# Softmax of a band attention before an MoE feed-forward: the guard becomes a second summed column, both query tiles are scaled by one reciprocal in one step, and the sink weights are copied out

## The chip, the cores and the metric

One core of one Trainium2 chip runs the whole kernel as a single launch. The metric is device time in microseconds of that core. The kernel before took 796.38, 807.41 and 798.26 us in three runs, median 798.26 us. The profiled execution took 798.38 us. Differences under about 2% (16 us) count as no change here.

## The reference, cut to what matters

```python
scores = scale * np.matmul(q, k.transpose(0, 1, 3, 2))        # 4 batches, 8 heads, 768 x 768, head size 64
keep = is_sink | in_window                                     # first 4 keys, or the last 128 keys
scores = np.where(keep, scores, -1000000000.0)
scores = scores - np.max(scores, axis=-1, keepdims=True)
a = np.exp(scores)
a = a / (np.sum(a, axis=-1, keepdims=True) + 1e-09)
attn = np.matmul(a, v)
x = attn.transpose(0, 2, 1, 3).reshape(3072, 512)
gate = 1.0 / (1.0 + np.exp(-(x @ w_gate)))                     # w_gate, w_val: 512 x 1536
out = (gate * (x @ w_val)) @ w_out                             # w_out: 1536 x 512
```

The inputs are float64 for the weights and float32 for q, k and v, and the result is float32. The kernel reads the float64 weights as pairs of 32-bit words and decodes them on the chip.

## The kernel before, in words

**Attention.** A unit is one batch, one head and T = 2 tiles of 128 query rows. There are 96 units, in the order batch, group of two tiles, head. For a query tile, a 128-wide band and 4 sink columns are kept, so a row of weights has KW = 132 columns. For each of the two tiles TensorE makes the scores (tile `a`), VectorE merges the two diagonal halves, adds the mask, scales and takes the row's extreme (`top`, line 743; it writes `P` and `negm_all`), and ScalarE takes the exponential of `P` in place with the row sums accumulated into `rs` (`exp`, line 751). Then for both tiles together the guard 1e-9 is added to `rs` (line 764, GpSimd or VectorE), VectorE takes the reciprocal (line 771), each tile's 128 band columns are multiplied by it (lines 773 to 789, GpSimd, ScalarE or VectorE), and the 4 sink columns of both tiles are multiplied into `psk`, which collects them over the 8 heads (line 792, VectorE or GpSimd). TensorE transposes the band part of `P` (`turn`, line 810), ScalarE copies it to `wt`, GpSimd splits it at the diagonal with two selects (`split`, line 816), and TensorE multiplies by `v` (`pv`, line 872). After the eighth head `join` (line 928) adds the sink part from `psk` and writes the split activations `XH` and `XL`, of which a ring of 6 tiles is kept. The first 16 units are "plain": they use unsplit float32 operands.

**Weights.** 36 `decode` steps (line 995) each load 512 KB of float64 words into `wst`, turn them into `w` by one ScalarE step, one conversion of `wst` on ScalarE, VectorE or GpSimd (line 1019) and two VectorE steps, and split `w` into a high part (`wgh`, `wvh`, `woh`) and a low one (`wgl`, `wvl`, `wlo`). The low part of the output weights goes to DRAM (`wol_d`) and is loaded again for each use (`wol`).

**Feed-forward.** `feed` (line 1061) takes chunks of 2 or 3 tiles of tokens. For each of the 12 slices of 128 hidden columns TensorE makes 12 matmuls for the gate and 12 for the value (into `m`), ScalarE takes the tanh (`th`), VectorE multiplies, `gh` and `gl` split the product, and 3 matmuls a tile accumulate into `o`.

**What sets the order.** Each step is put on a list with `plan.op` (line 264): a priority, the engines that may do it with a time in ns for each, and the tiles that it reads and writes. `Plan.run` (line 288) goes through a clock of its own, gives each free engine the first waiting step that it may do, and multiplies the times on VectorE, ScalarE and GpSimd by 1.2 before 200 us (line 393). The instructions are then emitted in that order, and each engine's order is kept. A step's time in the table so sets where it and all later ones stand, and on which engine. Where TensorE would stay too idle before 130 us, the plan puts a filler matmul (`m<-ident`, `warm`, line 649) into its queue. `P` and `rs` have two buffers, `a` has three.

Of the kernel before, what the change touches and what calls it, by code (L numbers as in the profile page):

```python
# [9 lines left out]
F32 = mybir.dt.float32  # L10
# [5 lines left out]
ALU = mybir.AluOpType  # L16
AX = mybir.AxisListType
# [3 lines left out]
NS = 4  # L21
# [50 lines left out]
BUFS = {}  # L72
# [361 lines left out]
def kernel(  # L434
# [13 lines left out]
    nc = tc.nc  # L448
# [11 lines left out]
    KW = 128 + NS  # L460
# [17 lines left out]
    plan = Plan()  # L478
# [72 lines left out]
    def tile(shape, dtype, tag, bufs, pool=None):  # L551
        return Tile(pool or p1, shape, dtype, tag, bufs)
# [89 lines left out]
    plan.op(-1, [("G", 250, places)], w=[mk])  # L642


    MS = [ps.tile([128, 512], F32, name=f"m{i}") for i in range(BUFS["m"])]
    assert max(map(max, MT)) * 128 + 128 <= 512
    PE.matmul(MS[0][:, 384:512], lhsT=ident, rhs=ident, start=True, stop=True)
# [44 lines left out]
    def attend(u, b, h, t0, T, XR, XS, PSK):  # L692
# [32 lines left out]
            PSK[0] = tile([128, T, H, NS], F32, "psk", BUFS["psk"])  # L725
        psk = PSK[0]
        P = tile([128, T, KW], F32, "P", BUFS["P"])
        rs = tile([128, 4], F32, "rs", BUFS["P"])
        for t in range(T):
            sc = tile([128, 512], F32, "a", BUFS["a"], ps)  # L730
            first = t0 + t == 0
            n = KW if first else KW + 128

            def qk(t=t, sc=sc, n=n):
                s0 = max(t + prev - 1, 0) * KW
                K = D if plain else 128
                for i, (qq, kk) in enumerate(pairs):
                    PE.matmul(
                        sc()[:, 0:n], lhsT=qq()[0:K, t * 128 : t * 128 + 128],
                        rhs=kk()[0:K, s0 : s0 + n], start=i == 0, stop=i == len(pairs) - 1,  # L740
                    )

            def top(t=t, sc=sc, first=first):
                if not first:
                    V.copy_predicated(out=sc()[:, 0:128], mask=tri, data=sc()[:, KW : KW + 128])
                V.tensor_tensor_reduce(
                    out=P()[:, t], in0=sc()[:, 0:KW], in1=am[min(t0 + t, 2)], op0=ALU.add,
                    op1=ALU.min, scale=-SCALE, scalar=3.0e38, accum_out=negm_all[:, u, t : t + 1],
                )

            def exp(t=t):
                A.activation(
                    out=P()[:, t], in_=P()[:, t], func=AF.Exp, bias=negm_all[:, u, t : t + 1],
                    scale=-1.0, accum_out=rs()[:, t : t + 1],
                )

            plan.op(u, [("PE", 90 + 1.667 * n if plain else 10 + 2 * mac(n), qk)], qk_reads, [sc, (P, t)], busy=0.5 if plain else 0.9)
            plan.op(
                u, [("V", 290 if first else 600, top)],
                [sc, (MASKS, 3), (MASKS, min(t0 + t, 2))], [sc, (P, t)],  # L760
            )
            plan.op(u, [("A", 460, exp)], [], [(P, t), (rs, t)])

        def guard(E):
            return lambda: E.tensor_scalar(
                out=rs()[:, 0:T], in0=rs()[:, 0:T], scalar1=1.0e-9, scalar2=None, op0=ALU.add
            )

        plan.op(u, [("G", 400, guard(G)), ("V", 250, guard(V))], [], [rs])
        plan.op(  # L770
            u, [("V", 120, lambda: V.reciprocal(out=rs()[:, 0:T], in_=rs()[:, 0:T]))], [], [rs]
        )
        for t in range(T):
            plan.op(
                u, [
                    ("V", 390, lambda t=t: V.tensor_scalar(
                        out=P()[:, t, 0:128], in0=P()[:, t, 0:128], scalar1=rs()[:, t : t + 1],
                        scalar2=None, op0=ALU.mult,
                    )),
                    ("A", 320, lambda t=t: A.mul(  # L780
                        out=P()[:, t, 0:128], in_=P()[:, t, 0:128], mul=rs()[:, t : t + 1]
                    )),
                    ("G", 450, lambda t=t: G.tensor_scalar(
                        out=P()[:, t, 0:128], in0=P()[:, t, 0:128], scalar1=rs()[:, t : t + 1],
                        scalar2=None, op0=ALU.mult,
                    )),
                ][::-1],
                [rs], [(P, t)],
            )


        def sink_weights(E):
            return lambda: E.tensor_tensor(
                out=psk()[:, 0:T, h], in0=P()[:, 0:T, 128:KW],
                in1=rs()[:, 0:T].unsqueeze(2).to_broadcast([128, T, NS]), op=ALU.mult,
            )

        plan.op(
            u, [("V", 110, sink_weights(V)), ("G", 400, sink_weights(G))], [rs, (P, T)], [(psk, h)]
        )  # L800


# [192 lines left out]
    def decode(prio, src, hi, lo):  # L995

        n, m = src.shape[1], src.shape[2]
        st = tile([128, n, m, 2], I32, "wst", BUFS["wst"], p2)
        a = tile([128, n, m], F32, "w2", BUFS["w2"])
        ai = lambda: a().bitcast(I32)
        hw = lambda: st()[:, :, :, 1]
        plan.op(prio, [("Q", 460, lambda: Q.dma_start(out=st(), in_=src))], [], [st], dma=1456.0)
        by = lambda i: st().rearrange("p n m w -> p (n m w)").bitcast(U8).rearrange(
            "p (x b) -> p x b", b=8
        )[:, :, i]
        plan.op(  # L1010
            prio, [("A", act(512), lambda: A.mul(out=a(), in_=hw().bitcast(F32), mul=2.0**-112))],
            [(st, 0)], [a],
        )

        lw = lambda: st()[:, :, :, 0]
        three = dict(scale=1.0 / 32, bias=-31.0 / 64)
        two = dict(scalar1=1.0 / 32, scalar2=-31.0 / 64, op0=ALU.mult, op1=ALU.add)
        flat = lambda: st().rearrange("p n m w -> p (n m w)").rearrange("p (x w) -> p x w", w=2)[:, :, 0]
        plan.op(
            prio, [  # L1020
                ("A", act(512), lambda: A.activation(out=flat(), in_=by(3), func=AF.Copy, **three)),
                ("V", 700.0, lambda: V.tensor_scalar(out=flat(), in0=by(3), **two)),
                ("G", 1000.0, lambda: G.tensor_scalar(out=flat(), in0=by(3), **two)),
            ],
            [], [(st, 1)],
        )
        plan.op(
            prio, [("V", vec(512), lambda: V.scalar_tensor_tensor(
                out=ai(), in0=ai(), scalar=3, in1=lw(), op0=ALU.logical_shift_left,
                op1=ALU.bitwise_or,  # L1030
            ))],
            [(st, 1)], [a],
        )
        plan.op(
            prio, [("V", vec(512), lambda: V.scalar_tensor_tensor(
                out=ai(), in0=hw(), scalar=-2147483648, in1=ai(), op0=ALU.bitwise_and,
                op1=ALU.bitwise_or,
            ))],
            [(st, 0)], [a],
        )  # L1040
        copy(prio, 512, hi, a, [a], [hi])
        rest(prio, 512, lo, a, hi, [a, hi], [lo])
# [210 lines left out]
```

## Time and profile before

| | |
|---|---|
| median of three runs | 798.26 us |
| profiled execution | 798.38 us, its span 796.7 us |
| TensorE matmul (PE) | busy 773.8 us, 97% of the span |
| VectorE (DVE) | 513.4 us, 64% |
| GpSimd (POOL) | 437.5 us, 55% |
| ScalarE (ACT) | 403.2 us, 51% |
| mean granted clock of TensorE | 0.992 of 2.4 GHz |

A share of the span is a mean over stages. The span begins 1.4 us before the first matmul and ends with the last store. The profile's time of a matmul runs from its start to its modelled end, and neighbours overlap, so a busy share of 1.0 says that TensorE had no gap, not how fast it streams. A filler counts as busy.

### The profile page before, as it was taken

To read this page: it belongs to the slowest core of one execution; us is meant where nothing else is said; L and a number is where in the kernel's file an instruction comes from. 1 tells how busy PE (TensorE), PEld (TensorE's weight loads), DVE (VectorE), ACT (ScalarE), POOL (GpSimd) and SP (SyncE) were. 2 spreads that over 40 slices of the span, in tenths; PEclk is the share of its full clock that TensorE was granted. 3 is DMA by queue.
4 is the path that set the end of the run, shared out by engine and by line. 5 is a ranking of instruction groups with operands and counts; after the bars stand their busy time and mean duration, and the time that the engine had idled before them with its cause. 6 is when DMAs were issued, how large, how long until landed. Compare 5 with 4: busy or idle time off the path is not lost. (4 is left out here: it accounts for less than half of the span.)

```text
span 796.7 us, 14763 instructions
## 1 busy us (share of the span) xinstructions
PE 773.8 (97%) x4540; PEld 702.8 (88%) x4540; DVE 513.4 (64%) x1550; ACT 403.2 (51%) x1190; POOL 437.5 (55%) x602
## 2 busy tenths in 40 slices
PE   7999999999999999999999999999999999999996
PEld 5677798878999999998999999999999999999995
DVE  5787798998799988899871388885861331111110
ACT  4786777766767767676640256664740210011001
POOL 3676798887667778668761267673751221111211
PEclk8999999999999999999999999999999999999999
DMA  5667777763645544444441235343311121113111
GB/s 162 198 190 207 191 213 253 231 201 115 192 126 151 149 107 122 119 116 112 142 113 40 57 104 133 104 129 111 92 45 42 41 79 40 40 40 92 39 42 57
DMA packets 98421, 94.33 MB, mean 118 GB/s; under 512 B 43168, under 2 KB 77984, under 8 KB 98336
## 3 DMA queue, kind: packets, MB, share of 16 engines
q1 hardware_dynamic: 98336, 93.32, 41.1%
q8 instruction: 38, 0.62, 0.3%
q14 instruction: 47, 0.39, 0.1%
HBM read 83.85 MB, written 9.44 MB: 117 GB/s over the span
## 5 line engine op out<-in xcount | busy, mean ns | idle before, releaser
L488 DVE SCALAR_TENSOR_TENSOR th<-th,m 128x384 f32<-128x384 f32 (+1 forms) x108 | 54.6, 505 | 184.3 <-PE m L488 182.9
L488 POOL TENSOR_TENSOR gl<-th,gh 128x384 fp32r<-128x384 f32 (+1 forms) x65 | 65.5, 1008 | 195.4 <-DVE gh L488 183.0
L488 ACT ACTIVATE th<-m 128x384 f32<-128x384 f32 (+1 forms) x108 | 49.1, 454 | 209.4 <-PE m L488 207.5
L488 POOL TENSOR_SCALAR_AFFINE_SELECT wt<-wt 128x512 fp32r<-128x512 f32 (+3 forms) x192 | 121.5, 633 | 42.6 <-DVE wt L488 24.2
L488 PE MATMUL m<-XH,wvh 128*128 128x384 f32 (+1 forms) x432 | 140.1, 324 | 0.4 <-ACT th L488 0.4
L488 PE MATMUL m<-XH,wgh 128*128 128x384 f32 (+1 forms) x432 | 140.3, 325 | 0.0
L488 PE MATMUL m<-XH,wvl 128*128 128x384 f32 (+1 forms) x432 | 137.7, 319 | 0.0
L488 PE MATMUL m<-XL,wvh 128*128 128x384 f32 (+1 forms) x432 | 137.6, 319 | 0.0
L488 PE MATMUL m<-XH,wgl 128*128 128x384 f32 (+1 forms) x432 | 137.5, 318 | 0.0
L488 PE MATMUL m<-XL,wgh 128*128 128x384 f32 (+1 forms) x432 | 137.3, 318 | 0.0
L488 PE MATMUL o<-woh,gh 128*128 128x512 f32 x276 | 113.0, 409 | 1.0 <-DVE total L1201 1.0
L488 PE MATMUL o<-woh,gl 128*128 128x512 f32 x276 | 109.5, 397 | 2.2 <-DVE gl L488 1.6
L488 PE MATMUL o<-wol,gh 128*128 128x512 f32 x276 | 108.8, 394 | 2.5 <-DMA wol<-wol_d 2.5
L488 ACT ACTIVATE P<-P,negm_all 128x132 f32<-128x132 f32 x192 | 77.2, 402 | 30.5 <-DVE negm_all L488 27.0
L488 PEld LDWEIGHTS m<-XH,wvh 128*128 128x128 f32 x432 | 81.7, 189 | 3.3 <-ACT th L488 0.6
L488 PEld LDWEIGHTS m<-XH,wgh 128*128 128x128 f32 x432 | 81.4, 189 | 2.1 <-issue 0.2
L488 PEld LDWEIGHTS m<-XL,wvh 128*128 128x128 f32 x432 | 81.8, 189 | 1.5
L488 PEld LDWEIGHTS m<-XL,wgh 128*128 128x128 f32 x432 | 81.5, 189 | 1.6
L488 PEld LDWEIGHTS m<-XH,wvl 128*128 128x128 f32 x432 | 81.7, 189 | 0.0
L488 PEld LDWEIGHTS m<-XH,wgl 128*128 128x128 f32 x432 | 81.3, 188 | 0.0
L488 PEld LDWEIGHTS o<-woh,gl 128*128 128x128 f32 x276 | 52.0, 188 | 16.6 <-DVE gl L488 3.5
L488 DVE CUSTOM_DVE_ANT_0 P<-a,am 128x132 f32<-128x132 f32 x192 | 56.2, 294 | 11.9 <-PE a L488 2.9
(115 smaller groups left out, 1619.5 us busy)
## 6 DMA issues: line engine op xcount, KB each, us to landing
wol<-wol_d SPq DMA_DIRECT2D x108, 256.0 KB, 2.7
qkT<-in_k_dram SPq DMA_DIRECT2D x120, 99.0 KB, 2.6
qkT<-in_q_dram SPq DMA_DIRECT2D x176, 64.0 KB, 2.4
wst<-in_moe_w_gate_dram SPq DMA_DIRECT2D x12, 512.0 KB, 4.3
wst<-in_moe_w_val_dram SPq DMA_DIRECT2D x12, 512.0 KB, 4.3
wst<-in_moe_w_out_dram SPq DMA_DIRECT2D x12, 512.0 KB, 4.2
vraw<-in_v_dram SPq DMA_DIRECT2D x64, 96.0 KB, 2.3
out_dram<-w SPq DMA_DIRECT2D x23, 256.0 KB, 2.5
```

The source lines that it names most:

```text
L488: return lambda *a, **kw: tc.keep_in_program_order(op(*a, **kw))
```

## The change

The guard is no longer added by an instruction. Two small tiles `sums` with two columns for each query tile are filled with 1e-9 once, before the plan begins; the exponential's accumulator overwrites the first column of a tile's pair, and one VectorE reduction adds both columns into `rs`, with the reciprocal right behind it in the same step. The scaling covers all 132 columns of both tiles: one instruction on GpSimd or VectorE, or two on ScalarE. The sink weights are then copied to `psk` by GpSimd or ScalarE. One time in the decode's table changes (GpSimd's conversion of `wst`, 1000 to 560 ns).

```diff
+    SUMS = [const.tile([128, 2, 2], F32, name=f"sums{i}") for i in range(BUFS["P"])]
+    for x in SUMS:
+        nc.gpsimd.memset(x, 1.0e-9)
...
-        rs = tile([128, 4], F32, "rs", BUFS["P"])
+        sums = Tile(SUMS, None, F32, "sums", BUFS["P"])
+        rs = tile([128, T], F32, "rs", BUFS["P"])
...
-                    scale=-1.0, accum_out=rs()[:, t : t + 1],
+                    scale=-1.0, accum_out=sums()[:, t, 0:1],
...
-        plan.op(u, [("G", 400, guard(G)), ("V", 250, guard(V))], [], [rs])
-        plan.op(
-            u, [("V", 120, lambda: V.reciprocal(out=rs()[:, 0:T], in_=rs()[:, 0:T]))], [], [rs]
-        )
-        for t in range(T):
...
-                    ("V", 390, lambda t=t: V.tensor_scalar(
-                        out=P()[:, t, 0:128], in0=P()[:, t, 0:128], scalar1=rs()[:, t : t + 1],
...
-                    ("A", 320, lambda t=t: A.mul(
...
-                    ("G", 450, lambda t=t: G.tensor_scalar(
...
-        plan.op(
-            u, [("V", 110, sink_weights(V)), ("G", 400, sink_weights(G))], [rs, (P, T)], [(psk, h)]
         )
+        def guard():
+            V.tensor_reduce(out=rs(), in_=sums()[:, 0:T], axis=AX.X, op=ALU.add)
+            V.reciprocal(out=rs(), in_=rs())
+
+        plan.op(u, [("V", 320, guard)], [sums], [rs])
+        def norm(E):
+            return lambda: E.tensor_tensor(
+                out=P(), in0=P(), in1=rs().unsqueeze(2).to_broadcast([128, T, KW]), op=ALU.mult
+            )
+        def norm_each():
+            for t in range(T):
+                A.mul(out=P()[:, t], in_=P()[:, t], mul=rs()[:, t : t + 1])
+        plan.op(
+            u, [("G", 800, norm(G)), ("A", T * 350, norm_each), ("V", 380, norm(V))], [rs], [P]
+        )
+        gather = lambda: psk()[:, 0:T, h]
+        plan.op(
+            u, [
+                ("G", 230, lambda: G.tensor_copy(out=gather(), in_=P()[:, :, 128:KW])),
+                ("A", 250, lambda: A.copy(out=gather(), in_=P()[:, :, 128:KW])),
+            ],
+            [P], [(psk, h)],
+        )
...
-                ("G", 1000.0, lambda: G.tensor_scalar(out=flat(), in0=by(3), **two)),
+                ("G", 560.0, lambda: G.tensor_scalar(out=flat(), in0=by(3), **two)),
```

Counted over the whole program, the order moves these. VectorE loses 80 sink products, 43 guards and 11 scalings, and gains 96 reductions, 13 scalings of both tiles and 5 conversions of `wst`. GpSimd loses 53 guards, 45 scalings and 16 sink products, and gains 31 scalings of both tiles and 39 sink copies. ScalarE has 104 scalings instead of 136, 57 sink copies and 6 conversions of `wst` fewer. Of other steps, 12 differences `kl` and 5 `gl` go from VectorE to GpSimd. TensorE has 66 fillers instead of 69, each of them two matmul records, and its other work is the same in number.

Of the first 29 units' work, VectorE loses 23 sink products, 10 guards and 4 scalings, and gains 29 reductions, 2 scalings of both tiles and the 5 conversions. GpSimd loses 19 guards, 11 scalings and 5 sink products, and gains 9 scalings of both tiles and 12 copies. ScalarE has 36 scalings instead of 41, 17 copies, and 14 conversions instead of 20.

VectorE at the first units, before (`ISA P` is the masked extreme, `tri` the merge mask, `wst` and `w` the decode):

```order
L488 ISA P_230,negm_all<-a_220,am_86 128x132
L488 ISA negm_all 128x1
L488 TENSOR_SCALAR wst_205<-wst_205 128x512
L488 COPY_PREDICATED a_228<-tri,a_228 128x128
L488 ISA P_230,negm_all<-a_228,am_87 128x132
L488 ISA negm_all 128x1
L488 RECIPROCAL rs_218<-rs_218 128x2
L488 SCALAR_TENSOR_TENSOR w_241<-w_241,wst_205 128x512
L488 TENSOR_TENSOR psk_255<-P_215,rs_218 128x2x4
L488 SCALAR_TENSOR_TENSOR w_241<-wst_205,w_241 128x512
```

and now:

```order
L488 ISA P_233,negm_all<-a_223,am_86 128x132
L488 ISA negm_all 128x1
L488 TENSOR_SCALAR wst_209<-wst_209 128x512
L488 TENSOR_REDUCE rs_245<-sums_90 128x2
L488 RECIPROCAL rs_245<-rs_245 128x2
L488 COPY_PREDICATED a_231<-tri,a_231 128x128
L488 ISA P_233,negm_all<-a_231,am_87 128x132
L488 ISA negm_all 128x1
L488 SCALAR_TENSOR_TENSOR w_242<-w_242,wst_209 128x512
L488 SCALAR_TENSOR_TENSOR w_242<-wst_209,w_242 128x512
L488 TENSOR_REDUCE rs_272<-sums_91 128x2
```

The first unit's reciprocal stands right behind the first conversion of `wst`, where the merge and the extreme of the second unit stood ahead of it before, and no sink product follows.

GpSimd at the same place, before (`vsp` belongs to the sink values, `wt` to the transposed weights):

```order
L488 TENSOR_TENSOR vsp<-w_190,vsp 32x512
L488 TENSOR_SCALAR rs_218<-rs_218 128x2
L488 TENSOR_SCALAR wst_209<-wst_209 128x512
L488 TENSOR_SCALAR wst_213<-wst_213 128x512
L488 TENSOR_SCALAR rs_234<-rs_234 128x2
L488 AFFINE_SELECT wt_267<-wt_267 128x128
L488 AFFINE_SELECT wt_267<-wt_267 128x2x128
```

and now:

```order
L488 TENSOR_TENSOR vsp<-w_194,vsp 32x512
L488 TENSOR_TENSOR P_219<-P_219,rs_245 128x264
L488 COPY psk_257<-P_219 128x2x4
L488 TENSOR_SCALAR wst_217<-wst_217 128x512
L488 AFFINE_SELECT wt_268<-wt_268 128x128
L488 AFFINE_SELECT wt_268<-wt_268 128x2x128
```

The guards are gone, the first unit's scaling has moved here from ScalarE, and one of two conversions has gone to ScalarE.

TensorE up to the second unit's transposes, before (`m_90<-ident` is the filler, `ident,P` the transposes of a unit, `qkT` the scores):

```order
L488 MATMUL m_90<-ident 128x128 x5
L488 MATMUL a_261<-ident,P_215 128x128 x2
L488 MATMUL a_265<-qkT_193 128x132
L488 MATMUL a_271<-qkT_193 128x260
L488 MATMUL m_90<-ident 128x128 x5
```

and now:

```order
L488 MATMUL m_94<-ident 128x128 x4
L488 MATMUL a_259<-ident,P_219 128x128 x2
L488 MATMUL m_94<-ident 128x128
L488 MATMUL a_266<-qkT_197 128x132
L488 MATMUL a_270<-qkT_197 128x260
L488 MATMUL m_94<-ident 128x128 x4
```

One filler has moved behind the first unit's transposes and one has gone.

## Rows read from the trace of the kernel before

**Rows 1.** The page's head, its busy times by engine, and two rows of its 40 slices of about 20 us: TensorE's busy tenths and the granted clock in tenths.

```profile
span 796.7 us, 14763 instructions
...
PE 773.8 (97%) x4540; PEld 702.8 (88%) x4540; DVE 513.4 (64%) x1550; ACT 403.2 (51%) x1190; POOL 437.5 (55%) x602
...
PE   7999999999999999999999999999999999999996
...
PEclk8999999999999999999999999999999999999999
```

**Rows 2.** Busy time of each engine in three stretches, with the number of instructions, the granted clock, the DMA engines' share and GB/s.

```profile
0.00:60.00 60.00, 53.18 (x291) 39.67 (x292) 44.12 (x153) 39.82 (x114) 34.38 (x59) 0.94 0.62 184
60.00:200.00 140.00, 132.47 (x876) 115.56 (x875) 122.88 (x295) 100.86 (x277) 114.46 (x130) 0.99 0.67 200
200.00:790.00 590.00, 587.62 (x3376) 547.45 (x3375) 346.37 (x1105) 261.33 (x800) 288.70 (x415) 1.00 0.34 92
```

**Rows 3.** What TensorE waited for between 60 and 200 us: us in total, times, longest.

```profile
PE o L488 <- DMA wol<-wol_d: 2.5, 2, 1.3
PE o L488 <- DVE gl L488: 1.6, 3, 0.7
PE a L488 <- DVE xr L488: 0.8, 2, 0.5
PE a L488 <- DVE negm_all L488: 0.7, 2, 0.4
PE a L488 <- DVE wt L488: 0.4, 1, 0.4
```

**Rows 4.** The fillers in the groups of instructions of the whole span (count of records, busy us, mean ns, idle before), and the stretch 80 to 90 us in the columns of Rows 2.

```profile
L488 PE MATMUL m<-ident 128*128 128x128 f32 x138 | 24.8, 320 | 1.6 <-POOL ident masks.py:199 1.4
...
80.00:90.00 10.00, 8.63 (x44) 6.71 (x44) 6.68 (x20) 6.13 (x20) 6.31 (x9) 0.83 0.83 221
```

**Rows 5.** VectorE's groups of the softmax's last steps between 0 and 200 us: count, busy us, mean ns, idle of the engine just before them and what ended it.

```profile
L488 DVE TENSOR_TENSOR psk<-P,rs 128x8 f32<-128x8 f32 x23 | 12.3, 536 | 0.0
...
L488 DVE TENSOR_SCALAR rs<-rs 128x2 f32<-128x2 f32 x10 | 4.6, 461 | 2.9 <-ACT P L488 2.9
L488 DVE RECIPROCAL rs<-rs 128x2 f32<-128x2 f32 x29 | 4.5, 156 | 0.9 <-POOL rs L488 0.8
...
L488 DVE TENSOR_SCALAR P<-P,rs 128x128 f32<-128x128 f32 x4 | 2.5, 636 | 0.0
```

**Rows 6.** GpSimd's groups of the same stretch, the same columns: the steps that go, and two differences of about the new scaling's size.

```profile
L488 POOL TENSOR_TENSOR qs<-qkT,qs 64x256 fp32r<-64x256 f32 x11 | 11.1, 1005 | 2.1 <-POOL wt L488 0.9 <-POOL vhl L488 0.5
...
L488 POOL TENSOR_SCALAR P<-P,rs 128x128 f32<-128x128 f32 x11 | 9.0, 824 | 2.8 <-DVE rs L488 1.7 <-ACT wst L488 1.0
...
L488 POOL TENSOR_SCALAR rs<-rs 128x2 f32<-128x2 f32 x19 | 6.4, 335 | 7.1 <-ACT P L488 6.1
...
L488 POOL TENSOR_TENSOR kl<-qkT,kh 128x264 fp32r<-128x264 f32 x3 | 2.3, 771 | 0.2
...
L488 POOL TENSOR_TENSOR psk<-P,rs 128x8 f32<-128x8 f32 x5 | 1.6, 326 | 1.3 <-DVE rs L488 1.3
```

**Rows 7.** ScalarE's groups of the same stretch, the same columns.

```profile
L488 ACT ACTIVATE P<-P,rs 128x128 f32<-128x128 f32 x41 | 15.0, 393 | 0.7 <-DVE rs L488 0.3
L488 ACT ACTIVATE wst<-wst 128x512 int32<-128x512 uint8 x20 | 13.6, 680 | 14.1 <-DMA wst<-in_moe_w_gate_dram 8.8 <-DMA wst<-in_moe_w_out_dram 4.1 <-DMA wst<-in_moe_w_val_dram 1.0
L488 ACT ACTIVATION_READ_ACCUMULATOR P<-P,negm_all 128x1 f32 x58 | 11.0, 190 | 0.0
...
L488 ACT CAST vhl<-vraw 128x128 fp32r<-128x128 f32 x2 | 0.6, 298 | 0.9 <-PE a L488 0.9
```

**Rows 8.** The timeline at the first unit: start in us, duration, engine, operation, and in brackets the idle time before it. VectorE, then ScalarE, then TensorE.

```profile
11.13 0.43 DVE L488 TENSOR_SCALAR wst<-wst 128x512 int32<-128x512 uint8 x1 [2.94 <-DMA wst<-in_moe_w_gate_dram]
11.47 0.29 DVE L488 COPY_PREDICATED a<-tri,a 128x128 f32<-128x128 int32 x1
...
12.02 0.16 DVE L488 RECIPROCAL rs<-rs 128x2 f32<-128x2 f32 x1
...
13.11 0.68 ACT L488 ACTIVATE P<-P,rs 128x128 f32<-128x128 f32 x2
...
8.12 1.38 PE L488 MATMUL m<-ident 128*128 128x128 f32 x10
13.55 0.77 PE L488 MATMUL a<-ident,P 128*128 128x128 f32 x2 [4.05 <-ACT P L488]
```

**Rows 9.** The timeline of VectorE at three small steps that each need the one before, and of one VectorE and one GpSimd instruction that ran side by side.

```profile
4.97 0.16 DVE L488 SCALAR_TENSOR_TENSOR val<-nums 128x2 f32<-128x2 f32 x1
5.17 0.17 DVE L488 TENSOR_SCALAR val<-val 128x2 f32<-128x2 f32 x1
5.37 0.35 DVE L488 SCALAR_TENSOR_TENSOR wst<-wst,val 128x128 f32<-128x128 f32 x1
...
16.69 1.39 DVE L488 TENSOR_SCALAR P<-P,rs 128x128 f32<-128x128 f32 x1
...
16.72 1.28 POOL L488 TENSOR_TENSOR wgl<-w,wgh 128x512 fp32r<-128x512 f32 x1
```

More of the change, by code (lines that the diff above doesn't have):

```diff
@@ L761, in attend @@
             )
[L762 to L766, printed above, removed]
-            )
-        plan.op(u, [("G", 400, guard(G)), ("V", 250, guard(V))], [], [rs])
+            plan.op(u, [("A", 460, exp)], [], [(P, t), (sums, t)])
+        def guard():
+            V.tensor_reduce(out=rs(), in_=sums()[:, 0:T], axis=AX.X, op=ALU.add)
+            V.reciprocal(out=rs(), in_=rs())
@@ L772, in attend @@
         )
-        for t in range(T):
-            plan.op(
-                u, [
-                    ("V", 390, lambda t=t: V.tensor_scalar(
-                        out=P()[:, t, 0:128], in0=P()[:, t, 0:128], scalar1=rs()[:, t : t + 1],
-                        scalar2=None, op0=ALU.mult,
-                    )),
-                    ("A", 320, lambda t=t: A.mul(
-                        out=P()[:, t, 0:128], in_=P()[:, t, 0:128], mul=rs()[:, t : t + 1]
-                    )),
-                    ("G", 450, lambda t=t: G.tensor_scalar(
[L784 to L788, printed above, removed]
-            )
@@ L792, in sink_weights @@
[L792 to L796, printed above, removed]
-        plan.op(
-            u, [("V", 110, sink_weights(V)), ("G", 400, sink_weights(G))], [rs, (P, T)], [(psk, h)]
+        gather = lambda: psk()[:, 0:T, h]
+        plan.op(
+            u, [
[3 more added lines that the diff above has]
+            [P], [(psk, h)],
```

## The prediction, made before the change was run

> **What bounds the kernel now.** I read the page first: TensorE is busy for 97% of the span and no other engine reaches two thirds [rows 1]. That leaves little to win anywhere, so the question is where TensorE's gaps lie. Its row of slices shows them in the first 200 us only, so the next view is the busy time by stretch [rows 2]. From 200 to 790 us TensorE has a matmul in hand for 587.62 of 590 us: 2.4 us of gaps, while VectorE works 346 us of it. In that stretch nothing off TensorE can be worth more than 2.4 us. From 60 to 200 us TensorE is idle for 140 - 132.47 = 7.5 us, and VectorE is the fullest of the others, 122.88 of 140 us (88%). From 0 to 60 us it is idle for 6.8 us, of which 4.05 us is one wait before the first unit's transposes [rows 8]. Besides idle time there are fillers, which count as busy and do nothing: 138 records with 24.8 us [rows 4]. So the most that a better supply could give back is 7.5 + 6.8 + 24.8 = 39 us, and a good part of that is loading and decoding of weights, which the change leaves alone. Who makes TensorE wait is read from its waits between 60 and 200 us [rows 3]: VectorE for 1.6 + 0.8 + 0.7 + 0.4 = 3.5 us, the reload of `wol` for 2.5 us; GpSimd is not among them.
>
> **The change, part by part.** The first 29 units are those of the first 200 us (29 reciprocals there [rows 5]); I cost these, and the other 67 at nothing: the 2.4 us of gaps after 200 us show that feed-forward matmuls cover them. If that cover went, VectorE's 346 us in 590 would still leave it room.
>
> *VectorE.* It loses 23 sink products (12.3 us), 10 guards (4.6) and 4 scalings (2.5) [rows 5]: 19.4 us. It gains 29 reductions, which no row shows. The nearest row is the reciprocal, one input of two columns, 0.156 us; but reduction and reciprocal now stand together and the second needs the first, and two such small steps start 0.20 us apart [rows 9]. I take 0.20, so 5.8 us. The ends are 0.156 (4.5 us) and 0.461, the guard's mean here (13.4 us). It further gains 2 scalings at 0.636 (1.3 us [rows 5]) and 5 conversions of `wst` at 0.43 (2.2 us [rows 8]). Net 10.1 us less of 44.12 + 122.88 = 167.0 us, between 2.5 and 11.4 less.
>
> Why the small steps cost so much is what the choice of 0.20 hangs on. The sink product took 0.536 us for 8 columns and the guard 0.461 for 2, while the reciprocal took 0.156 [rows 5]; and a scaling on VectorE that began beside a GpSimd subtraction lasted from 16.69 to 18.08 us, that subtraction from 16.72 to 18.00 [rows 9]. These steps wait for GpSimd, and the reciprocal does not. The Trainium skill, page "SBUF — State Buffer", section "Who interferes with whom", says that VectorE instructions with two inputs in SBUF or in a two-port mode block against GpSimd's, and that a reduction never does on trn2. By that rule the reduction costs as little as the reciprocal and the sum moves by 1.3 us on VectorE, which is nothing in the time; without it, at the guard's 0.461, the relief shrinks to 2.5 us. The trace agrees for the steps that go; no row shows a reduction beside a GpSimd instruction.
>
> *A wait that moves.* GpSimd added 19 of these 29 guards and stood idle for 7.1 us ahead of them, 6.1 of it for ScalarE's exponential [rows 6]. Now every guard is VectorE's, which stops its queue (the merges and extremes of the next unit, the decode, `gl`) until the second exponential is done. If all 6.1 us arrive there, the relief is 4.0 us, otherwise up to 10.1.
>
> *GpSimd* loses 6.4 + 9.0 + 1.6 = 17.0 us and gains 9 scalings of 264 columns, at 0.771 us by the nearest difference (6.9 us; 9.0 at 1.005), and 12 copies at 0.326 (3.9 us): 6.2 us less, at least 4.1 [rows 6]. *ScalarE* loses 5 scalings (2.0 us) and 6 conversions (4.1 us); 17 copies of 8 columns lie between 0.190, its shortest step, and 0.298, a cast of 128 columns; at 0.24 they are 4.1 us [rows 7]. Net 1.9 us less, between 0.9 and 2.8. I count both at nothing: TensorE waits for GpSimd nowhere in the waits shown [rows 3], and for ScalarE only at the start [rows 8].
>
> *The start.* TensorE stands from 9.50 to 13.55 us. The first weights land at 11.13; VectorE's conversion, merge and extreme come before the reciprocal at 12.02; ScalarE scales at 13.11 [rows 8]. Now the reduction is next after the conversion, which ends at 11.56; with 0.20 + 0.16 the reciprocal is done at about 11.92, and GpSimd, which has nothing else there, scales in 0.771: 12.7, with the hand-over 12.8. **0.75 us less.** The landing at 11.13 stays ahead of it, so the two memsets at the head, which delay fillers, cost nothing. The ends are 0 (GpSimd slower) and 1.5.
>
> *Fillers.* Three fewer, 6 records of 24.8 / 138 = 0.18 us [rows 4]: **1.1 us less**, if TensorE has work in their place; 0 if it waits instead.
>
> *What TensorE waits for on VectorE.* 3.5 us between 60 and 200 us [rows 3], with VectorE relieved by 4.0 to 10.1 us of 167.0, 2 to 6%. A few per cent off an engine that is 88% busy shortens these waits without ending them: I take half, **1.75 us less**, with ends 0 and 3.5. The waits for `wol` hang on the decode and a DMA and stay. What is late next where VectorE's waits go is that reload.
>
> The sum: 0.75 + 1.1 + 1.75 = 3.6 us, from the profiled execution's 798.4 us (1.7 us more than its span) to 794.8. That execution lies 0.1 us over the median of 798.26, so **795 us** stands for both. Its own range, by the ends above, is 790 to 798.5.
>
> **The rivals.**
>
> *The supply gets well* (chance 0.12). All 7.5 us of idle time between 60 and 200 us go, the reloads with them, because VectorE runs ahead of its plan; then also the fall of the clock at 80 to 90 us, where TensorE was idle for 1.4 us and the granted clock was 0.83 of 2.4 GHz (part of the stretch at 1.2 GHz), worth 0.17 x 10 = 1.7 us [rows 4]. 0.75 + 1.1 + 7.5 + 1.7 = 11.1 us: 787 us. For it: three engines lose work at once. Against it: the reload is the longest single cause and the change doesn't touch it.
>
> *The wait moves to VectorE* (chance 0.23), the one that ends slower. The reductions cost 0.461 as the guards did, and the 6.1 us of waiting arrive in front of them: VectorE then has 6.1 - 2.5 = 3.6 us more to spend, not less, in the stretch where it is 88% full. The decode queued behind it gets late by that much and TensorE waits for it, with one more fall of the clock (1.7 us): 798.4 + 5.3 = 804 us. It decides at the point where a reduction and the idle time ahead of it take over (10.1 + 5.8) / 29 = 0.55 us a unit. The old guards stood at 0.461 + 0.29 on VectorE [rows 5], and the idle time ahead of one on GpSimd was 7.1 / 19 = 0.37 us [rows 6]; with a reduction at 0.20 that makes 0.57, close to the point. Against it: the order puts other work ahead of a reduction where the plan expects a wait, and idle time on an engine that is 12% idle anyway isn't all lost.
>
> *Nothing moves* (chance 0.10). TensorE's gaps come from the landing of weights alone; the engines' relief is idle time: 798 us.
>
> **How the numbers follow.** My forecast has chance 0.55, so 795 us. The range goes from 787, where about half of the first rival is left out, to 804, where half of the second is; with the forecast's tails that leaves out about 2 in 10. Faster by over 2% (16 us, about what a measurement of this kernel can tell) means under 782.3 us: more than all idle time between 60 and 200 us and the start's gain together, so some of the fillers as well; 0.03. Slower by over 2% means over 814.3 us, three times the second rival's loss; 0.03. Within 2%: 0.94.
>
> **What would show it.** In the profile of the changed kernel: TensorE's first transposes at about 12.8 us with a wait of some 3.3 us; the reductions at 0.15 to 0.25 us each, not 0.46, and the idle time ahead of them under 0.35 us a unit; VectorE's busy time between 0 and 200 us about 10 us lower; GpSimd's scaling of 264 columns near 0.8 us, and ScalarE's sink copies between 0.19 and 0.3; 132 filler records; TensorE's waits for VectorE between 60 and 200 us under 3.5 us in sum; gaps after 200 us still near 2.4 us. I am wrong if TensorE shows new waits in that late stretch, if one of the first reductions holds VectorE for microseconds, or if the clock falls at a place where it didn't before.

## The result and the profile after

The changed kernel took 805.01 us (median of 20 runs, 799.02 to 810.09), the kernel before 798.82 us beside it (20 runs): ratio 1.0066, 95% interval 1.0045 to 1.0086. By the 2% bound that is no change; by the interval it is 0.4 to 0.9% slower, some 6 us, where I had forecast 3 us less. Single executions scatter: of the 20 of the kernel before 16 took 795.45 to 801.09 us and four 804.68 to 807.41, and the ratios and idle times below leave out executions over 1.5% above the fastest of their kernel. The profiled execution took 808.7 us, 3.7 us over its median, so its trace shows somewhat more lost time than the median run has.

The page's head, busy times and the two rows of slices that answer to [rows 1]:

```profile
span 807.0 us, 14725 instructions
...
PE 779.5 (97%) x4534; PEld 709.4 (88%) x4534; DVE 490.3 (61%) x1515; ACT 399.3 (49%) x1211; POOL 430.3 (53%) x574
...
PE   7999799998999999999999999999999999999996
...
PEclk8799999999999999999999999999999999999997
```

The three other engines have less to do, as the change says. TensorE's row has lower tenths (7, 8) where that of before had none, all in the first 200 us, and its clock is lower in the second slice (and in the last, from 798.3 us on). The stretches, as in [rows 2], say the same:

```profile
0.00:60.00 60.00, 52.70 (x256) 38.56 (x257) 37.23 (x141) 34.35 (x107) 29.69 (x54) 0.86 0.59 169
60.00:200.00 140.00, 128.84 (x838) 113.37 (x837) 113.10 (x276) 96.30 (x272) 105.25 (x113) 0.96 0.66 196
200.00:790.00 590.00, 588.53 (x3408) 550.35 (x3407) 339.00 (x1094) 266.41 (x829) 294.31 (x408) 1.00 0.34 94
```

From 60 to 200 us TensorE is idle for 11.16 us (7.53 before) and has 838 matmul records (876 before); after 200 us it has 1.47 us of gaps and catches nothing up. The loss is made before 200 us, and not only in that idle time: without the fillers (116 and 106 records up to 60 us, 22 and 26 from there to 200) TensorE has done 175 matmul records by 60 us in the kernel before and 150 in the changed one, and by 200 us 1029 and 962, of 4402 in either. So 25 of the 67 records that it is behind are missing at 60 us already. What TensorE waited for between 60 and 200 us, as in [rows 3]:

```profile
PE o L488 <- DMA wol<-wol_d: 5.3, 4, 2.0
PE a L488 <- POOL wt L488: 3.6, 1, 3.6
PE o L488 <- DVE gl L488: 0.8, 1, 0.8
PE a L488 <- ACT wt L488: 0.7, 1, 0.7
PE a L488 <- DVE sk L488: 0.3, 1, 0.3
```

VectorE's waits fell from 3.5 to 1.1 us, as forecast. In their place stand a longer wait for the reload of `wol` (5.3 us against 2.5) and one for GpSimd, which was not in the list before. The new steps themselves, in the groups of VectorE, GpSimd and ScalarE from 0 to 200 us (columns of [rows 5]), and the fillers of the whole span:

```profile
L488 DVE RECIPROCAL rs<-rs 128x2 f32<-128x2 f32 x27 | 4.5, 166 | 0.9
L488 DVE TENSOR_REDUCE rs<-sums 128x2 f32<-128x4 f32 x27 | 4.0, 148 | 1.3 <-ACT P L488 1.2
...
L488 POOL TENSOR_TENSOR P<-P,rs 128x264 f32<-128x264 f32 x8 | 6.0, 748 | 3.2 <-DVE rs L488 1.6 <-PE a L488 1.1 <-ACT w L488 0.3
...
L488 ACT COPY psk<-P 128x8 f32<-128x8 f32 x17 | 3.2, 191 | 1.0 <-POOL P L488 0.7
...
L488 PE MATMUL m<-ident 128*128 128x128 f32 x132 | 26.3, 342 | 1.7 <-POOL ident masks.py:199 1.7
```

All prices came out near the forecast: the reduction 0.148 us with 1.3 / 27 = 0.05 us of idle time ahead of it, the scaling of 264 columns 0.748, the copy 0.191. The start, as in [rows 8]:

```profile
10.87 0.43 DVE L488 TENSOR_SCALAR wst<-wst 128x512 int32<-128x512 uint8 x1 [2.50 <-DMA wst<-in_moe_w_gate_dram]
11.21 0.15 DVE L488 TENSOR_REDUCE rs<-sums 128x2 f32<-128x4 f32 x1
11.39 0.17 DVE L488 RECIPROCAL rs<-rs 128x2 f32<-128x2 f32 x1
...
11.73 0.62 POOL L488 TENSOR_TENSOR P<-P,rs 128x264 f32<-128x264 f32 x1 [1.59 <-DVE rs L488]
...
12.41 0.20 PEld L488 LDWEIGHTS a<-ident,P 128*128 128x128 f32 x2 [3.33 <-POOL P L488]
12.41 0.44 PE L488 MATMUL a<-ident,P 128*128 128x128 f32 x2 [3.14 <-POOL P L488]
```

The transposes start 1.14 us earlier than before, by the chain that I had described (0.26 us of it because the weights landed earlier). So every new step of the softmax took about the time that I had given it, and the kernel is slower. The largest new wait is this (GpSimd, VectorE, TensorE, then two rows of SP's queue):

```profile
93.00 0.64 POOL L488 TENSOR_SCALAR wst<-wst 128x512 int32<-128x512 uint8 x1 [4.63 <-DMA qkT<-in_q_dram]
93.71 0.88 POOL L488 TENSOR_SCALAR_AFFINE_SELECT wt<-wt 128x256 f32<-128x256 f32 x2
...
94.48 0.35 DVE L488 CAST vhl<-vraw 128x192 fp32r<-128x192 f32 x1 [4.27 <-DMA vraw<-in_v_dram]
...
94.65 1.54 PE L488 MATMUL a<-wt,vraw 128*64 128x256 f32 x6 [3.56 <-POOL wt L488]
...
88.20 0.53 SPq L488 DMA_DIRECT2D wst<-in_moe_w_val_dram  x1
...
103.39 0.34 SPq L488 DMA_DIRECT2D wst<-in_moe_w_out_dram  x1
```

In the new order a conversion of weights stands on GpSimd ahead of two selects. It waits for a load, the selects wait for it, and TensorE waits 3.56 us for them; behind that the clock falls to 1.2 GHz at 95.12 us for 3.4 us. Before, it fell at 84.06 us for as long, and at 12.38 us for 6.8; now it also falls at 132.66 and 194.1 us, and from 13.2 us on it stays at 1.2 GHz for 17.1 us. The conversion's row names a load of `q`, the last to land by the profile; its weights were issued at 88.20 us, and in the run below that moves this conversion the same wait is put down to them. The next load of weights went out only at 103.39 us.

### The profile page after: what moved, and what is told of

The parts are those of the page before. It is cut to its first block, busy times and chain, and to the rows that moved or that the text cites. A ratio compares the mean times of both kernels' runs of the same rounds, so it can differ in the third digit from the quotient of the medians.

```text
span 807.0 us, 14725 instructions
## 1 busy us (share of the span) xinstructions
PE 779.5 (97%) x4534; PEld 709.4 (88%) x4534; DVE 490.3 (61%) x1515; ACT 399.3 (49%) x1211; POOL 430.3 (53%) x574
## 5 line engine op out<-in xcount | busy, mean ns | idle before, releaser
L488 POOL TENSOR_TENSOR gl<-th,gh 128x384 fp32r<-128x384 f32 (+1 forms) x70 | 69.0, 986 | 198.8 <-DVE gh L488 169.6
L488 PE MATMUL o<-wol,gh 128*128 128x512 f32 x276 | 110.7, 401 | 6.3 <-DMA wol<-wol_d 6.3
```

Of the source, the lines that this page charges most:

```text
L488: return lambda *a, **kw: tc.keep_in_program_order(op(*a, **kw))
```

## The experiments

Each kernel was timed in five rounds beside the kernel before, on the same chip, with 6 to 13 executions each. "Idle" is TensorE's idle time from 60 to 200 us in the profiled execution (7.53 us in the kernel before, 11.16 in the changed one). The expectations weigh these causes: the clock at the start, the new steps on VectorE's queue, the new order of the work (by the shorter price or by the softmax's steps), the end of the decode, single waits.

**The clock at the start.** More fillers in both kernels, in the gaps before the first units' transposes and products; the order of all else is kept:

```diff
+FILL_T = {0: 13, 1: 3, 2: 3}   # kernel before: {0: 17, 1: 3, 2: 3}
+FILL_V = {0: 12, 1: 3, 2: 3}   # kernel before: {0: 4, 1: 3, 2: 3}
...
         def turn():
+            for _ in range(FILL_T.get(u, 0)):
+                warm()
...
         def pv():
+            for _ in range(FILL_V.get(u, 0)):
+                warm()
```

> The changed kernel with 37 more fillers in TensorE's queue ahead of the first three units' transposes and products with v, where TensorE waits anyway. Nothing else changes, and every engine's order is the same. Theory 1: the clock stays up from 6 us on, instead of falling for 17 us at 13 us, so the start is about 5 us shorter in the profiled run and the median comes down from 805 to 799 to 802. Rival (the start is bound by the loads and by the chain of the softmax, and the clock there costs nothing): 804 to 806 us, with the first feed-forward matmul at the same time.

> The kernel before with 33 more fillers at the same places, as a control. The clock there fell for 6.8 us at 12.4 us. Theory 1: at most 3.4 us are to be had, so 795 to 798 us. Rival (fillers do nothing, or cost their own 7 us): 799 to 805 us.

The changed kernel with fillers: 1.007 (1.0034 to 1.0105), the kernel before with them: 0.9986 (0.9951 to 1.002). The first stretch of the changed kernel with fillers:

```profile
0.00:60.00 60.00, 56.44 (x339) 44.62 (x340) 38.82 (x143) 34.62 (x110) 29.98 (x54) 0.97 0.60 174
```

The granted clock rose from 0.86 to 0.97 and the time moved in neither kernel. The fourth unit's transposes began at 27.73 us with these fillers and at 30.38 without, but the 20th's at 115.25 and 115.36 (in the kernel before at 114.85 and 114.84): what the clock brought at the start is gone by then, and TensorE goes there at the pace of what it is fed. The clock at the start is refuted as the cause of the distance. Nor do the later falls carry it: up to 215 us TensorE ran at 1.2 GHz for 10.2 us in the changed kernel with fillers, as in the kernel before (10.2), and this execution took 806.28 us against 798.38.

**The price alone, and the softmax alone with a new order.**

```diff
# kernel before
-                ("G", 1000.0, lambda: G.tensor_scalar(out=flat(), in0=by(3), **two)),
+                ("G", 560.0, lambda: G.tensor_scalar(out=flat(), in0=by(3), **two)),
# changed kernel: the same line back to 1000.0
```

> The kernel before with one number changed: GpSimd's conversion of wst priced 560 instead of 1000 ns. The softmax is the old one. Theory 1 (the extra 6 us are time at the lower clock and late reloads of wol, which any reshuffle of the order can bring or spare, and the softmax's new steps cost nothing by themselves): this number alone moves the time by something like the change does, 2 to 8 us either way of 798.8, with a granted clock that moves with it. Rival (the softmax's steps cost the time): 797 to 801 us, clock 0.99.

> The changed kernel with the conversion's price put back to 1000 ns, so the softmax's part of the change alone. Theory 1: anywhere from 793 to 806 us, and what it is goes with the clock: 0.99 gives at most 799, 0.98 gives 804 or more. Theory 2 (the conversion that the lower price puts on GpSimd waits for its load ahead of the selects, as at 93 us in the changed kernel, where TensorE stood 3.6 us): that wait is gone and the time is 799 to 801 us. Rival (the softmax's steps cost the time): 804 to 806 us.

The price alone: 1.0082 (1.0045 to 1.0119), idle 10.86 us. The softmax with the old price: 1.0071 (1.0035 to 1.0107), idle 9.91. Either half of the change costs as much as the whole. If each had its own price, both together would have to cost about twice as much, so what they share is suspect: each makes a new order.

**The softmax's steps in the old order.** The table of steps, its prices and so the order stay those of the kernel before, and only what is issued at a step's place is changed. First the guard as second column, with the reduction ahead of the reciprocal; then also both tiles scaled in one step; then also the sink copies (over all 132 columns, as in the change):

```diff
-                out=rs()[:, 0:T], in0=rs()[:, 0:T], scalar1=1.0e-9, scalar2=None, op0=ALU.add
+            return lambda: None
...
+            V.tensor_reduce(
+                out=rs()[:, 0:T], in_=SUMS[rs.slot][:, 0:T], axis=AX.X, op=ALU.add
+            )
             V.reciprocal(out=rs()[:, 0:T], in_=rs()[:, 0:T])
...
+        def scale(E):
+            scaled.append(E)
+            if len(scaled) < T:
+                return
...
+            if E is G:
+                return lambda: G.tensor_copy(out=gather(), in_=P()[:, :, 128:KW])
+            return lambda: A.copy(out=gather(), in_=P()[:, :, 128:KW])
```

> The kernel before with the guard column alone, in the old order: the plan and its prices are untouched, the old guard's step issues nothing, and the reciprocal's step issues the reduction of the two columns and then the reciprocal. Theory 3 (the new steps are cheap, and the loss comes from the order, which lets the weights be decoded later): 796 to 799 us, decode ends at 183 to 186 us after the span's start, as before (185.3). Rival (the guard on VectorE, with its wait for the exponential, costs the time): 802 to 806 us.

> As the one with the guard column alone, and the scaling of both query tiles is issued at one place: at the second of the two old steps, on its engine, over the 128 band columns (one instruction on GpSimd or VectorE, two on ScalarE); the sink product stays as before. The old order otherwise. Theory 3: 796 to 800 us. Rival (the joint scaling or the guard costs the time): 802 to 806 us.

> All of the changed softmax in the unchanged order of the kernel before: reduction and reciprocal where the reciprocal stood, both tiles scaled over 132 columns where the second scaling stood, and the sink weights copied out where the sink product stood (by ScalarE at the 80 places that were VectorE's, by GpSimd at its 16); prices and due times as before. If the loss hangs on the new order alone, this runs as the kernel before, 796 to 801 us, ratio 0.996 to 1.003, with TensorE's lost time before 220 us near the kernel before's 50 us. If the sink copies on ScalarE, the one part not yet tried in the old order, bring the loss, it runs at 803 to 806 us. If the relief of VectorE (80 sink products of 0.54 us fewer) is worth what I forecast, it falls to 796 or less.

Guard column alone: 0.9982 (0.9942 to 1.0022). With joint scaling: 1.000 (0.9967 to 1.0034). All of it: 1.0023 (0.999 to 1.0057); where the old order has the sink step ahead of the scaling, that kernel copies weights that are not scaled yet, so its time is read for the instructions alone. The stretches of the last:

```profile
0.00:60.00 60.00, 52.51 (x283) 39.41 (x284) 41.70 (x147) 39.33 (x119) 28.68 (x51) 0.94 0.62 178
60.00:200.00 140.00, 131.48 (x877) 114.77 (x876) 121.46 (x288) 102.30 (x293) 107.04 (x117) 1.00 0.68 203
```

GpSimd is relieved by 13.1 us in 200 and VectorE by 3.8 (against [rows 2]), and TensorE's idle time is 8.52 us and its records 877, close to the 7.53 and 876 of the old order. The new steps neither cost nor bring anything that this measurement shows; the last interval leaves room for up to 0.6%.

VectorE's relief is so small because other steps took it up. The softmax's last steps fell there by 14.3 us up to 200 us, but the two steps of each decode (36 of each) took longer, 0.980 and 0.920 us on the mean:

```profile
L488 DVE SCALAR_TENSOR_TENSOR w<-wst,w 128x512 int32<-128x512 int32 x36 | 35.3, 980 | 0.3
L488 DVE SCALAR_TENSOR_TENSOR w<-w,wst 128x512 int32<-128x512 int32 x36 | 33.0, 920 | 1.2 <-ACT w L488 1.2
```

In the kernel before they took these, 8.9 us less in sum:

```profile
L488 DVE SCALAR_TENSOR_TENSOR w<-w,wst 128x512 int32<-128x512 int32 x36 | 29.8, 830 | 0.0
L488 DVE SCALAR_TENSOR_TENSOR w<-wst,w 128x512 int32<-128x512 int32 x36 | 29.6, 822 | 0.1
```

What made them longer, no run here separates.

**Any new order.** Due times of the decode moved (earlier in the changed kernel, later in the one before), or one number of a step's price by 5 to 10 ns, in each kernel:

```diff
-DS1 = 6.0        # changed kernel 5.0, kernel before 7.0
-DS2 = 18.0       # changed kernel 16.0, kernel before 20.0
...
-        u, [("V", 120, lambda: V.reciprocal          # kernel before
+        u, [("V", 125, lambda: V.reciprocal
-        plan.op(u, [("V", 320, guard)], [sums], [rs])   # changed kernel
+        plan.op(u, [("V", 330, guard)], [sums], [rs])
-        plan.op(u, [("A", 460, exp)]                   # either kernel
+        plan.op(u, [("A", 465, exp)]
```

> The changed kernel with the weights due earlier in the plan (two numbers: the first slice due at unit 5 instead of 6, the fifth at 16 instead of 18). Theory 3 (the span follows the end of the decode, about 0.75 us for each us, since TensorE has no gaps after it: 185.3 gave 796.7, 199.0 gave 807.0): the decode ends at 185 to 192 us and the time comes to 797 to 802 us. Rival (the clock and the reloads of wol set it): 804 to 808 us whatever the decode does.

> The kernel before with the weights due later (the first slice at unit 7 instead of 6, the fifth at 20 instead of 18), nothing else. Theory 3: the decode ends 6 to 15 us later than 185.3 and the time grows by three quarters of that, 803 to 810 us, with the old softmax. Rival: within 797 to 801 us.

> The kernel before with one number of its table of times changed, the reciprocal's 120 to 125 ns; the instructions are the same, their order differs from about 30 us on. Theory 'any new order loses' (the times of the table had been fitted to this very order): 802 to 806 us, ratio 1.004 to 1.009, as after every other new plan tried here, with TensorE's lost time before 220 us at 54 to 58 us instead of 50. Theory 'the loss belongs to the change' (its shorter price of the conversion, its new steps): 797 to 800 us, ratio 0.998 to 1.002.

> The kernel before with another single number changed, the exponential's 460 to 465 ns. The same two theories as for the reciprocal's number: 802 to 806 us (ratio 1.004 to 1.009) if the old order was a well-fitted one and any new one loses; 797 to 800 us (0.998 to 1.002) if the loss belongs to the change. If one of these two loses and the other doesn't, orders scatter by some 5 us around the change's loss, and one order of each kernel can't tell the change's own worth.

> The changed kernel with one number of its table moved, reduction with reciprocal 320 to 330 ns; same instructions, another order. Theory 'orders scatter, and that of before was fitted': 802 to 810 us, ratio to the kernel before 1.003 to 1.015, as the new orders of the kernel before. Theory 'the change's order was unlucky': 799 us or less, ratio 1.000 or under.

> The changed kernel with another single number moved, the exponential's 460 to 465 ns; same instructions, another order. The same two theories as for the other number: 802 to 810 us (ratio 1.003 to 1.015) if orders scatter above a fitted one, 799 us or less if the change's own order was unlucky.

| kernel, what is moved | ratio, 95% interval | idle, us |
|---|---|---|
| changed, due times earlier | 1.0087 (1.0042 to 1.0132) | 13.48 |
| before, due times later | 1.0069 (1.0045 to 1.0093) | 11.82 |
| before, reciprocal 125 | 1.018 (1.0136 to 1.0223) | 13.66 |
| before, exponential 465 | 1.0062 (1.0033 to 1.0092) | none |
| changed, reduction 330 | 1.0097 (1.0059 to 1.0134) | 13.19 |
| changed, exponential 465 | 1.0116 (1.0069 to 1.0164) | none |

This decides it. Five nanoseconds in the planner's table, with no instruction changed, cost the kernel before 0.6% and 1.8%. Counting the change itself, nine new orders were timed, and all nine lie between 1.006 and 1.018, those of the old instructions and those of the new alike. The order of before stands some 5 to 14 us below all of them. The end of the decode alone is not what counts: with later due times its last VectorE step ended later (195.1 us) and the kernel was slower, as that theory said, but with earlier due times it ended at 180.3 us, before the 185.3 us of the kernel before, and the kernel was slower too. Where the time goes differs from order to order; the kernel before with the reciprocal at 125 has these two as its longest waits from 60 to 220 us:

```profile
PE m L488 <- DVE XL L488: 3.8, 1, 3.8
PE o L488 <- DVE a L488: 2.7, 1, 2.7
```

**Is it one wait?** In the changed order the conversion at 93.00 us, the ninth on GpSimd, is issued on ScalarE:

```diff
-                ("G", 560.0, lambda: G.tensor_scalar(out=flat(), in0=by(3), **two)),
+                ("G", 560.0, third),
...
+            if len(COUNT) == 9:
+                A.activation(out=flat(), in_=by(3), func=AF.Copy, **three)
```

> The changed kernel, but its ninth GpSimd conversion of weights (the one that starts at 93.00 us, waits 4.63 us for its load and stands ahead of two selects for which TensorE waits 3.56 us) is put on ScalarE at the same place; the rest of the order stays. Theory 'one convoy': this wait, the fall of the clock at 95 us behind it and the weight loads that go out late cost most of the 6 us; then the time falls by 3 to 6 us to 799 to 802 us (ratio to the kernel before 1.000 to 1.004) and the wait at 94.65 us is gone. Theory 'spread': the loss is spread over the 200 us in which weights are decoded, other waits take its place (the reload of the low output weights above all), and the time stays at 804 to 806 us, ratio 1.005 to 1.008.

```profile
93.60 0.67 ACT L489 ACTIVATE wst<-wst 128x512 int32<-128x512 uint8 x1 [4.29 <-DMA wst<-in_moe_w_val_dram]
94.17 0.34 ACT L489 COPY wt<-a 128x256 f32<-128x256 f32 x1
...
94.57 0.58 PE L489 MATMUL a<-kh,qs 128*128 128x260 f32 x1 [5.43 <-ACT wt L489]
```

1.0058 (1.0025 to 1.0092), no change. The wait only moved: now ScalarE's copy of `wt` stands behind the conversion, and TensorE waits 5.43 us for it. So this doesn't say what the kernel would be without that wait; it says that the conversion starts at about 93 us (93.00 there, 93.60 here), whichever engine does it. The next pair lets the loads land sooner.

**Late landings of weights.** A load lands when its last bytes are in the buffer. From the fifth load on, half of each weight load's bytes (the rest of the buffer keeps old words), same order and same work on every engine:

```diff
+            if len(WLOADS) <= 4:
+                Q.dma_start(out=st(), in_=src)
+            elif n > 1:
+                Q.dma_start(out=st()[:, 0 : n // 2], in_=src[:, 0 : n // 2])
+            else:
+                Q.dma_start(out=st()[:, :, 0 : m // 2], in_=src[:, :, 0 : m // 2])
```

> The changed kernel, order and work of every engine kept, but from the fifth on a weight load moves only half of its 512 KB (the other half of the buffer keeps old words, so those weights are not the reference's, and the buffers are allocated once). Theory 'landing': the new order loses because weight loads that land late (4 to 5 us after issue, three engines idle beside them) hold TensorE; with half the bytes the waits of 3.6 us at 94.65 us and most of the conversions' waits for loads go, and the kernel drops by 5 us or more, to 800 us or less, and comes within 2 us of the kernel before with half loads. Theory 'engines': the waits come from the order of work on the engines; it drops by less than 2 us and stays 5 us or more above the kernel before with half loads.

> The kernel before with the same cut of the weight loads to half their bytes from the fifth on. Theory 'landing': it has fewer such waits to lose, so it drops by less than the changed kernel does, to 795 to 799 us, and the two come within 2 us of each other. Theory 'engines': 797 to 800 us, and the changed kernel with half loads stays 5 us or more above it.

The changed kernel: 799.89 us, 1.000 (0.9974 to 1.0027). The kernel before: 793.26 us, 0.9934 (0.9897 to 0.9971). Each gains 5 us, and the distance between them stays, 6.6 us. The half loads land 2.9 to 3.2 us after their issue (medians by matrix) where the whole ones took 4.0 to 4.6, and in the changed kernel the wait of 4.63 us falls to 2.50 and TensorE's of 3.56 us behind it to 1.4. The stretch from 60 to 200 us of the changed kernel with half loads, and then of the kernel before with them:

```profile
60.00:200.00 140.00, 132.15 (x892) 116.33 (x891) 125.11 (x293) 102.02 (x289) 112.23 (x122) 1.00 0.53 157
```

```profile
60.00:200.00 140.00, 134.05 (x909) 118.49 (x909) 125.34 (x306) 104.07 (x286) 116.52 (x135) 1.00 0.56 166
```

Half of the weights' bytes cost both kernels the same 5 us. Late landings aren't what parts them.

**The reload of `wol`.** Left out after the first load of each buffer, in both (the matmuls then use those first low parts throughout):

```diff
-            pr, 728.0, lambda: Q.dma_start(out=wol().bitcast(F32), in_=wol_d[f]),
+            pr, 728.0, lambda: wol.tag in KEPT or Q.dma_start(out=wol().bitcast(F32), in_=wol_d[f]),
```

> The changed kernel, order kept, without the reloads of the low output weights after the first of each buffer (the matmuls take the first slice's low part for all slices, so the output differs a little from the reference's). Theory 'reload': the distance of 6 us to the kernel before is TensorE's longer wait for these reloads; the changed kernel drops by 5 us or more, to 800 us or less, and stands within 2 us of the kernel before without reloads. Theory 'order of the engines' work': the waits for the reload hide other work that is late as well; it drops by less than 4 us and stays 4 us or more above the kernel before without reloads.

> The kernel before without the same reloads. Theory 'reload': it has 2.5 us of such waits to lose and comes to 795 to 798 us, within 2 us of the changed kernel without reloads. Theory 'order of the engines' work': it comes to 794 to 799 us as well, but the changed kernel stays 4 us or more above it.

The changed kernel: 802.97 us, 1.005 (1.0008 to 1.0092). The kernel before: 796.63 us, 0.9987 (0.9968 to 1.0006). The distance stays at 6.3 us again, though the changed kernel's interval is wide. Its longest waits from 60 to 220 us are then:

```profile
PE a L488 <- POOL wt L488: 4.8, 2, 3.8
PE a L488 <- DVE xr L488: 0.9, 1, 0.9
```

The reload's waits are gone, and the wait for GpSimd and others that stood beside them remain.

**What stays open.** The new steps in the old order cost nothing that can be seen, and new orders of the old steps lose about as much as the change, or more: that the loss goes with the order is shown, and that the clock, late weight loads and the reload, each by itself, don't carry it. Which property of the old order makes it 5 us or more better than nine others is not: no single wait carries it in the kernels tried. That nine of nine new orders lose would fit an old order picked as the best of many; how the old order came about is not in these runs. A changed kernel whose own order fits as well was not found; the old order with the new steps says what it could be expected to give, 1.0023 (0.999 to 1.0057).

## Why the prediction was wrong

*The step that failed* is in the sum: I priced the new kernel by the waits of the old order. "I count both at nothing: TensorE waits for GpSimd nowhere in the waits shown", "The waits for `wol` hang on the decode and a DMA and stay", and half of VectorE's 3.5 us as a gain, all read [rows 3] as if the steps would keep their neighbours. The price that goes from 1000 to 560 ns had no term at all. The trace of the changed kernel has GpSimd with 3.6 us and `wol` with 5.3 us in that list, and the run with the price alone lost 0.8%. What the runs put in the place of this step is that an order has a price of its own: nine new orders lost 0.6 to 1.8%, 5 to 14 us, where my terms gave 3.6 us of gain.

*Right, and worth nothing.* Prices of reduction, scaling and copies, the first transposes (12.41 us for 12.8), 132 filler records, VectorE's waits under 3.5 us, no new gaps after 200 us. The 0.75 us at the start were even 1.14, but the run with fillers shows that the first units go at the pace of their supply. VectorE's busy time up to 200 us fell by 16.7 us, more than the 10 that I had named, but for 27 units' reductions and not 29. The fillers' 1.1 us did not come: fewer records, but 26.3 us instead of 24.8; 22 of them lie in the 17.1 us at 1.2 GHz.

*The relief* of VectorE (1.75 us) is the term that the runs in the old order price alone: nothing that can be seen. It failed a step earlier than in the waits: of the 10.1 us that I had taken off VectorE's 167.0 (12.3 without the conversions, which the old order doesn't move), 3.8 arrived there, because I had left the other steps at their old times and the decode's took 8.9 us more. What the whole relief would have been worth was not measured. On the choice of 0.20 us for the reduction: 0.148 us was measured, with GpSimd at work for 135 of the 200 us, and all 96 reductions took 0.135 to 0.159. The Trainium skill, page "SBUF — State Buffer", section "Who interferes with whom", says that a reduction on VectorE doesn't block against GpSimd on trn2; the trace agrees, by these times.

*Slips in the sum.* By the ends that I gave (0 to 1.5, 0 to 1.1, 0 to 3.5 us) the forecast's own range is 792.3 to 798.4 us, not 790 to 798.5. And TensorE did wait for ScalarE between 60 and 200 us, 0.4 us for `th`. Neither changes the account.

*The rivals.* "The wait moves to VectorE" gave 804 us, 1 us from the median, by a mechanism that didn't occur: a reduction and the idle time ahead of it take 0.20 us, not 0.55. "The supply gets well" is refuted: idle time grew. "Nothing moves" is, within the interval, what the steps alone do. The case that came true, that a new order is worse by itself, I had not among the rivals, and so the range ended 1 us below the result. One sign that I had named for being wrong did appear: the clock fell at new places (95, 133 and 194 us).

## What to carry to other kernels

Where a program lays out its order from a table of prices, any edit of that table is a draw of a new order: time two or three neighbours of it (a price moved by a few ns) before you credit or blame the instructions. Price the new steps apart from the order, by issuing them at the old steps' places. And read a list of waits as belonging to one order: an engine that isn't in it may be there in the next.

## What the runs showed of the hardware

With fillers TensorE's granted clock stayed near 2.4 GHz through the first 40 us (1.00 in the stretches 0 to 20 and 20 to 40 us, against 0.83 and 0.74), and the time did not change: the ratio is 1.007 with fillers and 1.0066 without. In the kernel before the first 60 us went from 0.94 to 1.00, at a ratio of 0.9986 (0.9951 to 1.002). So the 17.1 us at 1.2 GHz from 13.2 us on cost nothing that can be seen here, where TensorE went at the pace of its supply. Of longer stretches, or of others, this says nothing.

Halving the weight loads gave 5 us to a kernel whose DMA engines were busy for 0.67 of the stretch from 60 to 200 us ([rows 2], 0.56 with half loads): a mean share well under 1 does not say that the loads cost nothing. Whether the weights' earlier landing brought it, or the room that other transfers then had, was not separated.
